# Moving loads of raw W and pieces of a mixture within the first passes of a linear-attention and expert-mixture kernel

## The chip, the cores and the metric

The kernel runs on one core of a Trainium2 chip. The metric is the device time of one execution in microseconds; the time before is the median of three runs. The profiles show one execution each. Engine names are those of the profile: PE (TensorE matmuls), PEld (its weight loads), DVE (VectorE), ACT (ScalarE), POOL (GpSimd), SP (the engine that issues most DMAs; "SPq" rows are these issues).

## The reference

There are two stages. The first is a linear-attention recurrence over 768 tokens, for 4 batches and 8 heads of width 40. The second is a mixture of 4 experts, applied to each of the 3072 rows of 320 that the first stage gives.

```python
# r, k, v, w, a, b: [4, 8, 768, 40] float32; state: [4, 8, 40, 40]
for t in range(S):
    y[:, :, t] = einsum('bhd,bhde->bhe', r_t, state)
    Sa = einsum('bhde,bhe->bhd', state, a_t)
    state = state * w_t[:, :, None, :] - einsum('bhd,bhe->bhde', Sa, b_t) \
            + einsum('bhd,bhe->bhde', v_t, k_t)
x = y.transpose(0, 2, 1, 3).reshape(3072, 320)
p = probs / (probs.sum(-1, keepdims=True) + 1e-9)          # [3072, 4]
for e in range(4):
    h = maximum(x @ w1[e], 0)                              # w1[e]: 320 x 1024
    out += p[:, e:e+1] * (h @ w2[e])                       # w2[e]: 1024 x 320
```

## The kernel before, in words

**Units and passes.** Time is cut into 12 chunks of 64 tokens. A unit is one chunk of two batches (8 heads each), so there are 24 units, u = 0 to 23. After a prologue, a loop runs passes u = 1 to 23. In the words of the change a pass is counted from one: its "fifth pass" is u = 4, "pass 6" is u = 5, and "passes 6 to 8" are u = 5, 6, 7. This text says u throughout.

**What is made of a unit.** Three generators hold its work, and a pass advances several units at once:
- `within(unit)` has all that needs no state. Raw W is turned into `G` by two DVE transposes (`turn_raw`, L241), and a scan (L419) makes running products of it. These four short DVE instructions and their scan are called the G group here. Then `pg` on PE, `gp` and its reciprocal on DVE, `n_tok`, `k_tok`, `AT` (turned from raw A), `VT` and `RT` (from raw V and raw R), and on PE `pNT`, `pKT`, `pc`, `pfe`, `pe`; DVE masks the results into `VC` and `ET`, ACT copies `F`. Its last part is `E V`, the PE group `pev`, which reads `ET`.
- `substitute` inverts triangular blocks. ACT and DVE copy `blocks` from `F`, DVE turns them into `M` (L547, 2 us), and for units from 2 on POOL runs the substitution on `Z` (L572, L585). `merge` then turns `Z` into `Qc` and `QTc` on DVE (L596, L598) and finishes the inverse with `pY` and `pQ` on PE; the last of this is what the change calls the inverse product.
- `step(unit)` is the part with the state: `prn`, then `psat`, `pxr` and `pdy` on PE, the state's update on DVE, and at the end the rows x of the mixture, transposed, as `xT`. From chunk 2 on xT is placed by twelve SBUF-to-SBUF DMAs (L736) that SP issues.

**The mixture.** Chunk 0 is done unit by unit (`mixture_of_unit`), later chunks by two units at a time (`mixture_of_chunk`, 256 rows). Each is a list of entries in `todo`: `ups` computes h = relu(x w1) of one half of an expert, `down` or `down_1` and `down_2` multiply by w2. `ups` works on a piece of w1, loaded by three DMAs (L300) into one of two buffers `w1p` (some into `sums`), and consists of `up_last` (the last 64 of the 320 channels: 8 small matmuls, PE tile names `ph`) and `up_main` (the other 256; also `ph`), after which ACT takes both PSUM tiles through the relu (L770). The second product uses seven half-size products instead of eight: `add_h` forms five sums of h on DVE (`a`, L880), and PE makes `p431` in `down_1`, and `p75` and `p26` in `down_2` (all "p" in the profile). DVE adds these into `osb` (L784, L786), with `gate` and `minus_gate`.

**PSUM.** All `ph`, `po` and `p` tiles have one tag, `mm`, with three buffers that go round. A `ph` pair takes two of them, `p431`, `p75` and `p26` one each, so the second `ph` tile after a `p75`, `p26` pair takes the buffer of that `p75`. The attention's tiles have another tag with five buffers.

**What sets the order.** `gap(n)` calls `mix`, which runs the next one or two entries of `todo`; with `pieces` given it runs that many. `lead()` runs the `up_last` of the next entry ahead of its time if that entry has a `lead`. After the program is written, a scheduler orders each engine's instructions by its own costs, except those kept in program order; `in_order[0]` keeps all matmuls of a pass in program order. In passes with `early` (u below EARLY = 5) the order of the parts is another than later. Each engine's queue is then fixed and runs in order, SP's with its DMA issues too.

**Raw W.** `load_raw(unit, "W")` makes four DMA issues into a single buffer for all units, `rawW`; the next unit's may start when DVE has turned the one before. In pass u it is for unit u + 3.

The lines in question, in the loop:

```python
        if u + 3 < NU:
            go(load_raw(begin(u + 3), "WA"))
            load(units[u + 3], "WBKV")
            later.extend(load_raw(units[u + 3], "VR"))
```

Of the kernel before, what the change touches and what calls it, by code (L numbers as in the profile page):

```python
# [15 lines left out]
def kernel(  # L16
# [41 lines left out]
    E, DM, F = moe_w1.shape  # L58
    P = 128
# [5 lines left out]
    NU = NC * B // 2  # L65
    DT = DM - 2 * P

    in_order = [False]
# [6 lines left out]
    def matmul(**k):  # L75
        return stated(nc.tensor.matmul(**k))  # L76
# [104 lines left out]
    EARLY = 5  # L181
# [4 lines left out]
    units = []  # L186

    def begin(u):
        q = Unit()
        q.u, q.c, q.bp = u, u // (B // 2), u % (B // 2)  # L190
        q.b = [2 * q.bp, 2 * q.bp + 1]
        q.start, q.end = q.c == 0, q.c == NC - 1
        q.apart = u >= EARLY + 2
        q.n = {}
        units.append(q)
        return q
# [9 lines left out]
    def load_raw(q, names):  # L206


        moves = []
        for x in names:  # L210
            q.n["raw" + x] = t = raw[x]()
            heads = srcs[x].rearrange("b h t e -> (b h) t e")[q.b[0] * H:(q.b[1] + 1) * H, q.c * L:(q.c + 1) * L, :]
            heads = heads.rearrange("n (x two) e -> x n (two e)", two=2)
            for r in range(2):
                if x in "RV":

                    sets = ((slice(0, 8, 2), slice(r, 16, 4)), (slice(1, 8, 2), slice(3 - r, 16, 4)))
                else:
                    sets = ((slice(0, 8), slice(r, 16, 2)),)
                for n, hs in sets:  # L220
                    for y, w_ in enumerate((D + Q, 2 * D - Q)):
                        o = slice(64 * r + Q * y, 64 * r + Q * y + Q)
                        moves.append(lambda eng, out=t[o, n, 0:w_], in_=heads[:, hs, Q * y:Q * y + w_]: eng.dma_start(out=out, in_=in_))  # L223
        return moves
# [10 lines left out]
    def go(moves, eng=None):  # L235
        for move in moves:
            move(eng or nc.sync)
# [65 lines left out]
    def used(n):  # L303

        while len(pieces) < n_pieces:
            k = len(pieces)
            if k in in_sums:
                before = k - 5 if k >= 5 else -1
            else:
                at = [x for x in range(k) if x not in in_sums]  # L310
                before = at[-2] if len(at) > 1 else -1
            if before >= n:
                break
            load_piece()

    def load_w2(e):
        tc.keep_in_program_order(nc.sync.dma_start(out=w2_sb[e][:], in_=moe_w2[e].rearrange("(f p) d -> p f d", p=P)))
# [425 lines left out]
    def up_last(k, xT, n):  # L743

        w1 = pieces[k]
        ph = [ps.tile([P, HF // 2, n], FP32, name="ph", tag="mm", bufs=3) for _ in range(2)]

        for f in range(HF // 2):
            for c in range(2):
                for i in range(2):  # L750
                    matmul(
                        out=ph[i][half(c), f, :], lhsT=w1.last[part(i), f, half(c)],
                        rhs=xT[part(i), 2, :], start=(f == 0), stop=False,
                    )
        return ph

    def up_main(k, xT, n, ph):

        w1 = pieces[k]
        h = sb.tile([P, HF, 2 * P], FP32, name="hs", tag="hs", bufs=3)  # L760
        for i in range(2):
            for f in range(HF // 2):
                for g in range(2):
                    at = i * HF // 2 + f
                    matmul(
                        out=ph[i][:, f, :], lhsT=w1.main[:, g, at * P:(at + 1) * P],
                        rhs=xT[:, g, :], start=False, stop=(g == 1 and f == HF // 2 - 1),
                    )
        for i in range(2):
            nc.scalar.activation(  # L770
                out=h[:, i * HF // 2:(i + 1) * HF // 2, 0:n], in_=ph[i][:], func=ACTF.Relu,
            )
        return h

    def up(k, xT, n):
        return up_main(k, xT, n, up_last(k, xT, n))

    def scale(q, e, minus=False):
        return (minus_gate if minus else gate)[:, q.c, q.bp, e:e + 1]

# [15 lines left out]
    def mixture_of_unit(q):  # L796

        hs, at = {}, 2 * E * q.u

        def ups(e):  # L800
            hs[e] = [up(at + 2 * e + x, q.xT, P) for x in range(2)]
            used(at + 2 * e + 2)
            if q.u == 0 and e + 2 < E:
                load_w2(e + 2)

        def down(e):
            po = ps.tile([P, DM], FP32, name="po", tag="mm", bufs=3)
            for f in range(NF):
                matmul(
                    out=po[:], lhsT=hs[e][f // HF][:, f % HF, 0:P], rhs=w2_sb[e][:, f, :],  # L810
                    start=(f == 0), stop=(f == NF - 1),
                )
            if e == 0:
                q.osb = outputs()
            add(q.osb[:], po[:], scale(q, e), e == 0)
            if e == E - 1:
                stores.append(lambda: store(q, q.osb))

        todo.append(lambda: ups(0))
        for e in range(E):  # L820
            todo.append(lambda e=e: down(e))
            if e + 1 < E:
                todo.append(lambda e=e: ups(e + 1))

# [119 lines left out]
    todo, last, later, stores = [], [], [], []  # L946

    def begin_later(n):
        for move in later[:n]:
            tc.keep_in_program_order(move(nc.sync))  # L950
        del later[:n]

    def mix(n):

        for piece in todo[:n]:
            ready = stores[:]
            del stores[:]
            piece()
            for begin_store in ready:
                begin_store()  # L960
            begin_later(3 if n > 1 else 6)
        del todo[:n]

    def lead():
        if todo and hasattr(todo[0], "lead"):
            todo[0].lead()

    def run(gen, n=99):
        if gen is None:
            return  # L970
        for _ in range(n):
            if next(gen, gen) is gen:
                break
# [95 lines left out]
    sparse = range(4 * 1, 4 * 4 + 2)  # L1069
# [2 lines left out]
    sums_at.update({4 * 4 + 3: 2, 4 * 5 + 0: 3, 4 * 5 + 1: 2, 4 * 5 + 2: 3})  # L1072
    sum_ops = (None for e in range(E) for _ in add_weights(e))
    for u in range(1, NU):
        in_order[0] = u < EARLY
        q = units[u]
        m = s_next = w = w_next = iter(())
        if u + 1 < NU:
            m, s_next = merge(units[u + 1]), begin_step(u + 1)
            w_next = ws[u + 1]  # L1080
        if u + 2 < NU:
            w = ws[u + 2]

        def gap(n, pieces=None):
            at = 4 * u + n
            run(sum_ops, sums_at.get(at, 0))
            mix((1 if at in sparse else 2) if pieces is None else pieces)

        early = u < EARLY
        if early:  # L1090
            begin_later(len(later))
        run(w_next, 99 if early else 1)
        run(s, 1)
        gap(0)


        if early:
            run(s, 1)
        run(w, 1)
        if not early:  # L1100
            run(w_next)
            run(s)

        if early:
            run(w, 1)
            gap(1)
            run(s)
        if u == 1:
            mixture_of_unit(q)
        elif q.bp:  # L1110
            mixture_of_chunk(units[u - 1:u + 1], chunks_x[q.c])
        if not early:
            begin_later(len(later))
            run(w, 1)
            run(m, 1)
            gap(1)

        if u + 3 < NU:
            go(load_raw(begin(u + 3), "WA"))
            load(units[u + 3], "WBKV")  # L1120
            later.extend(load_raw(units[u + 3], "VR"))
        run(w, 2)

        soon = u in (2, 3, 4)
        if soon:
            run(w, 1)
        if early:
            run(m, 1)
        else:
            run(s_next, 1)  # L1130
            run(m, 1)
        if soon:
            substitute(units[u + 2], nc.gpsimd)
        gap(2)

        if not early:
            run(m, 1)
        if not soon:
            run(w, 1)
        if not early:  # L1140
            lead()
            run(s_next, 1)
        if not soon and u + 2 < NU:
            substitute(units[u + 2], nc.gpsimd)
        if early:
            run(w, 1)
        if u + 3 < NU:
            ws.append(within(units[u + 3]))
            run(ws[u + 3], 1)
        if early:  # L1150
            run(m, 1)
            run(s_next, 1)
            run(m)
            gap(3, 1)
            run(s_next, 1)
            mix(0 if 4 * u + 3 in sparse else 1)
        else:
            gap(3)
        s = s_next
# [31 lines left out]
```

## Time and profile before

| | us |
|---|---|
| median of three runs (1123.12 to 1125.46) | 1123.36 |
| the profiled execution | 1122.36 |
| its span, first to last instruction | 1120.2 |
| PE busy | 1076.8 |
| DVE busy | 757.0 |
| POOL busy | 501.9 |
| ACT busy | 353.2 |
| mean granted PE clock | 0.986 |

The span is what the views divide; the profiled execution is 2.16 us longer than its span. Shares of busy time are averages over the whole span, and a busy PE is not PE at its peak. A row of the timeline gives start, duration, engine, line, operation, out<-in and shapes; in brackets stands the idle time of the engine just before, and what ended it. A row of the windows view gives a stretch, its length, and for each engine its busy time in it and the number of instructions, then the mean PE clock, the DMA share and GB/s. Passes begin on PE at about 95 us (u = 1), 129 (u = 2), 161 (u = 3), 191 (u = 4), 233 (u = 5), 280 (u = 6), 329 (u = 7) and 372 (u = 8); from there on a pass takes about 43 us.

### The profile page before, as it was taken

How to read it: one execution, taken by the hardware profiler on the slowest of the kernel's cores; microseconds unless marked ns; L12 is line 12 of the kernel's file. 1: busy time of each engine (PE TensorE's matmuls, PEld its weight loads, DVE VectorE, ACT ScalarE, POOL GpSimd, SP SyncE). 2: the span in 40 equal slices, each digit the busy share in tenths (PEclk: the TensorE clock that was granted, in tenths of full speed). 3: DMA queues.
4: the chain of work that ended last, by engine and by line, in shares of the span. 5: the costliest groups of instructions: out<-in, count | busy, mean ns of one | idle time of the engine just before them, and what ended most of it. 6: DMA issues, size and time to landing. Idle time of an engine off the chain costs nothing.

```text
span 1120.2 us, 38531 instructions
## 1 busy us (share of the span) xinstructions
PE 1076.8 (96%) x16100; PEld 961.0 (86%) x16100; DVE 757.0 (68%) x1553; ACT 353.2 (32%) x956; POOL 501.9 (45%) x1272
## 2 busy tenths in 40 slices
PE   6888899898989999999999999999999999999998
PEld 5777777787978989989999998989989899988887
DVE  8665588886657767767767677677677686543343
ACT  2322444233332332333332432342332333321110
POOL 5004676761625635636536437437346346340000
PEclk8899999999999999999999999999999999999999
DMA  7785536335353454553544543543543542231330
GB/s 116 203 250 139 124 68 152 80 95 121 81 110 93 122 126 97 130 123 82 128 99 101 129 107 86 143 100 88 143 106 87 129 103 64 77 90 60 107 90 12
DMA packets 268869, 122.18 MB, mean 109 GB/s; under 512 B 213737, under 2 KB 242073, under 8 KB 268697
## 3 DMA queue, kind: packets, MB, share of 16 engines
q1 hardware_dynamic: 265416, 119.12, 44.0%
q8 instruction: 127, 2.08, 0.8%
q10 hardware_dynamic: 3280, 0.61, 0.3%
q14 instruction: 46, 0.37, 0.1%
HBM read 111.79 MB, written 3.93 MB: 103 GB/s over the span
## 4 chain that ended last, share of the span: by engine, by line
PE 59%; POOL 12%; DVE 9%; issue 5%; ACT 4%; SPq 2%; DMA 2%; DVEq 0%; POOLq 0%
PE ph L76 26%; PE p L76 20%; POOL Z L585 8%; POOL Z L572 4%; PE psat L76 2%; PE pdy L76 2%; DVE M L547 1%; SPq L223 1%; PE pxr L76 1%; PE po L76 1%; PE pfe L76 1%; PE pQ L76 1%; DVE G L419 1%; ACT Yq L619 1%; PE prn L76 1%
## 5 line engine op out<-in xcount | busy, mean ns | idle before, releaser
L76 PE MATMUL ph<-xT,w1p 128*128 128x256 f32 (+3 forms) x3040 | 446.0, 378 | 7.8 <-issue 7.8
L76 PEld LDWEIGHTS ph<-xT,w1p 64*64 64x64 f32 (+1 forms) x3040 | 338.3, 162 | 76.6 <-issue 33.8
L585 POOL TENSOR_TENSOR Z<-Z 128x31 f32<-128x31 f32 (+7 forms) x704 | 259.1, 368 | 55.2
L880 DVE TENSOR_TENSOR a<-hs 128x512 f32<-128x512 f32 x220 | 152.3, 710 | 105.9 <-ACT hs L770 105.9
L572 POOL TENSOR_TENSOR Z<-M,Z 128x62 f32<-128x62 f32 (+7 forms) x352 | 145.8, 414 | 139.0 <-DVE M L563 113.2
L770 ACT ACTIVATE hs<-ph 128x512 f32<-128x512 f32 (+1 forms) x208 | 115.0, 564 | 214.5 <-PE ph L76 213.4
L76 PE MATMUL p<-sums,a 128*128 128x160 f32 x1056 | 164.8, 299 | 0.0
L76 PEld LDWEIGHTS p<-sums,a 128*128 128x128 f32 x1056 | 152.9, 190 | 2.2
L786 DVE SCALAR_TENSOR_TENSOR osb<-p,gate,osb 128x320 f32<-128x320 f32 (+1 forms) x243 | 108.1, 482 | 60.3 <-PE p L76 56.9
L544 POOL COPY below<-F 32x256 f32<-32x256 f32 x48 | 24.0, 501 | 221.0 <-ACT F L502 219.5
L76 PE MATMUL p<-w,a 128*128 128x160 f32 x704 | 106.2, 301 | 1.3 <-ACT hs L770 0.8
L76 PE MATMUL p<-w,hs 128*128 128x160 f32 x704 | 102.9, 299 | 0.0
L76 PEld LDWEIGHTS p<-w,a 128*128 128x128 f32 x704 | 98.3, 190 | 4.4 <-ACT hs L770 4.4
L76 PEld LDWEIGHTS p<-w,hs 128*128 128x128 f32 x704 | 100.2, 190 | 2.2
L604 POOL COPY QT<-QTc 32x256 f32<-32x256 f32 x96 | 50.3, 524 | 75.2 <-DVE QTc L598 35.1
L547 DVE STREAM_TRANSPOSE M<-blocks 128x1024 f32<-128x1024 f32 x24 | 47.3, 1971 | 39.5 <-ACT blocks L541 39.4
L692 ACT COPY RS<-pxr 64x256 f32<-64x256 f32 x88 | 32.4, 368 | 108.5 <-DVE SX L400 43.3
L529 ACT COPY EV<-pev 64x160 f32<-64x160 f32 x96 | 23.5, 287 | 93.4 <-PE pev L76 93.0
L432 DVE RECIPROCAL gp<-gp 128x320 f32<-128x320 f32 x24 | 51.6, 2151 | 0.7
L596 DVE STREAM_TRANSPOSE Qc<-Z 128x256 f32<-128x256 f32 x24 | 15.0, 627 | 46.4 <-POOL Z L585 46.3
L619 ACT COPY QT<-pQ 32x128 f32<-32x128 f32 x96 | 24.7, 257 | 58.9 <-PE pQ L76 57.2
L651 ACT COPY SN<-prn 128x256 f32<-128x256 f32 x44 | 15.0, 371 | 80.4 <-DVE RH L646 77.6
(147 smaller groups left out, 1371.0 us busy)
## 6 DMA issues: line engine op xcount, KB each, us to landing
w1p<-in_moe_w_dram SPq DMA_DIRECT2D x95, 512.0 KB
w1p<-in_moe_w_dram SPq DMA_DIRECT2D x190, 64.0 KB
w<-in_moe_w_dram SPq DMA_DIRECT2D x4, 1280.0 KB
sums<-in_moe_w_dram SPq DMA_DIRECT2D x9, 512.0 KB
natW<-in_w_dram SPq DMA_DIRECT2D x48, 80.0 KB
natB<-in_b_dram SPq DMA_DIRECT2D x48, 80.0 KB
natK<-in_k_dram SPq DMA_DIRECT2D x48, 80.0 KB
out_dram<-osb SPq DMA_DIRECT2D x46, 80.0 KB
```

Of the source, the lines that this page charges most:

```text
L76: return stated(nc.tensor.matmul(**k))
L432: pin(nc.vector.reciprocal(out=gp[:], in_=gp[:]))
L544: tc.keep_in_program_order(nc.gpsimd.tensor_copy(out=q.below[quarter(i)], in_=q.F[quarter(i), :, 0:Q]))
L547: ins = nc.vector.transpose(out=M[:], in_=cols)
L572: ins = eng.tensor_tensor(out=Z[:, 1:3, 0:n, j + 1:Q], in0=M[:, j:j + 2, None, j + 1:Q].to_broadcast([P, 2, n, m]), in1=Z[:, here, 0:n, j: ...
L585: eng.tensor_tensor(out=z[:, 0], in0=z[:, 0], in1=z[:, x], op=ALU.add)
L604: ins = nc.gpsimd.tensor_copy(out=q.QT[quarter(i), :, quarter(i % 2)], in_=QTc[quarter(i)])
L619: nc.scalar.copy(out=of_slot(to[quarter(2 * r)], y), in_=src)
L692: nc.scalar.copy(out=RS[half(s), x ^ s::2], in_=prs[x][half(s)].rearrange("p (j i) t -> p j i t", i=2),)
L770: nc.scalar.activation(out=h[:, i * HF // 2:(i + 1) * HF // 2, 0:n], in_=ph[i][:], func=ACTF.Relu,)
L786: nc.vector.scalar_tensor_tensor(out=to, in0=p, scalar=sc, in1=to, op0=ALU.mult, op1=ALU.add)
L880: nc.vector.tensor_tensor(out=t[:], in0=x, in1=y, op=op)
```

## The change

- For u = 5, 6, 7 raw W of unit u + 3 is begun at the head of the pass; raw A keeps its place.
- In the unit-wise mixture `ups` becomes an entry with a `lead`, and for u = 1 to 4 `lead()` is called at the head of the pass. This puts the next piece's `up_last` ahead of `pev`.
- In u = 4 `gap(1)` runs two entries instead of one, and the one entry at the end of that pass is dropped.
- `in_order` holds for u = 5 too.

```diff
-    def up(k, xT, n):
-        return up_main(k, xT, n, up_last(k, xT, n))
-
...
         def ups(e):
-            hs[e] = [up(at + 2 * e + x, q.xT, P) for x in range(2)]
-            used(at + 2 * e + 2)
-            if q.u == 0 and e + 2 < E:
-                load_w2(e + 2)
+            ph = []
+
+            def lead():
+                if not ph:
+                    ph.append(up_last(at + 2 * e, q.xT, P))
+
+            def piece():
+                lead()
+                hs[e] = [up_main(at + 2 * e, q.xT, P, ph[0])]
+                hs[e].append(up_main(at + 2 * e + 1, q.xT, P, up_last(at + 2 * e + 1, q.xT, P)))
+                used(at + 2 * e + 2)
+                if q.u == 0 and e + 2 < E:
+                    load_w2(e + 2)
+
+            piece.lead = lead
+            return piece
...
-        todo.append(lambda: ups(0))
+        todo.append(ups(0))
         for e in range(E):
             todo.append(lambda e=e: down(e))
             if e + 1 < E:
-                todo.append(lambda e=e: ups(e + 1))
+                todo.append(ups(e + 1))
...
-        in_order[0] = u < EARLY
+        in_order[0] = u <= EARLY
...
         if early:
             begin_later(len(later))
+        ahead = u + 3 < NU and u in range(EARLY, EARLY + 3)
+        if ahead:
+            go(load_raw(begin(u + 3), "W"))
+        if early:
+            lead()
         run(w_next, 99 if early else 1)
         run(s, 1)
         gap(0)
...
         if early:
             run(w, 1)
-            gap(1)
+            gap(1, 2 if u + 1 == EARLY else None)
             run(s)
...
         if u + 3 < NU:
-            go(load_raw(begin(u + 3), "WA"))
+            go(load_raw(units[u + 3] if ahead else begin(u + 3), "A" if ahead else "WA"))
             load(units[u + 3], "WBKV")
             later.extend(load_raw(units[u + 3], "VR"))
...
             gap(3, 1)
             run(s_next, 1)
-            mix(0 if 4 * u + 3 in sparse else 1)
         else:
             gap(3)
```

In the order as built, these moves show:
- On PE, from u = 1 to u = 4, eight `ph` matmuls stand before `pev` instead of after `pxr`. In u = 4 a whole `ph` piece stands before `pNT` instead of after `pfe`, the next one before `pY` instead of before `psat`, and `p431` before `psat` instead of after it. From the `ph` in u = 5 on PE's order is the same.
- On DVE, in u = 5, 6, 7, the G group stands right after `k_tok`, ahead of `RT` and `Qc`, instead of after the additions to `w` and `sums` (u = 5), after `RH` (u = 6) and around `QTc` (u = 7).
- On SP, the four issues of raw W stand before the weight piece that precedes the second half of raw R. In u = 4 the three issues of one weight piece stand in front of the last three of the twelve xT issues.
- POOL's order is the same.

## Prediction

> **What bounds the kernel now.** I read the page first: engine totals, clock row, and the chain that ended last.
>
> ```profile
> PE 1076.8 (96%) x16100; PEld 961.0 (86%) x16100; DVE 757.0 (68%) x1553; ACT 353.2 (32%) x956; POOL 501.9 (45%) x1272
> ...
> PE 59%; POOL 12%; DVE 9%; issue 5%; ACT 4%; SPq 2%; DMA 2%; DVEq 0%; POOLq 0%
> ```
>
> PE is busy 96% of the span, so this kernel gets shorter only where PE stands still or runs at half clock. I therefore listed PE's idle stretches in the timeline. Between 90 us and the end, those of over 0.4 us, but for one of 0.44 at 489, all lie before 364 us, in u = 1 to 7, the passes that the change touches. Then I asked for the busy time of each engine in the stretches with a gap, and in one like the late ones without a gap (406.27 to 415.18, u = 8):
>
> ```profile
> core 0: us, PE busy (x) PEld busy (x) DVE busy (x) ACT busy (x) POOL busy (x), PEclk, DMA share, GB/s
> 94.00:98.80 4.80, 2.14 (x69) 1.49 (x70) 4.55 (x10) 0.24 (x2) 1.31 (x5) 1.00 0.60 160
> ...
> 160.64:163.94 3.30, 2.87 (x161) 2.63 (x164) 0.55 (x1) 2.05 (x8) 2.67 (x9) 1.00 0.05 11
> ...
> 201.30:221.27 19.97, 16.80 (x198) 15.14 (x196) 19.17 (x36) 4.19 (x9) 13.62 (x35) 0.91 0.37 81
> 265.88:279.90 14.02, 11.01 (x130) 9.55 (x122) 10.75 (x19) 5.11 (x15) 2.85 (x7) 0.88 0.66 150
> 313.51:328.58 15.07, 11.02 (x131) 9.52 (x123) 10.98 (x19) 5.11 (x16) 2.06 (x5) 0.89 0.52 125
> 362.19:372.40 10.21, 9.43 (x131) 8.23 (x123) 7.24 (x13) 5.11 (x15) 2.38 (x5) 1.00 0.65 157
> 406.27:415.18 8.91, 8.91 (x134) 8.10 (x127) 5.80 (x10) 5.16 (x16) 1.83 (x5) 1.00 0.60 134
> ```
>
> The rows from 265.88, 313.51 and 362.19 hold the instructions of the last row (`ph`, `psat`, `ph`, `p`) in u = 5, 6, 7: 14.02, 15.07 and 10.21 us instead of 8.91. The excess is 5.1, 6.15 and 1.3 us, part PE standing still, part PEclk below 1. The page calls the releaser "issue", so I followed the first in the timeline:
>
> ```profile
> 249.18 9.80 SPq L736 DMA_DIRECT2D xT<-Y  x12
> ...
> 259.08 1.65 SPq L300 DMA_DIRECT2D w1p<-in_moe_w_dram  x3
> 260.77 1.56 SPq L223 DMA_DIRECT2D rawW<-in_w_dram  x3
> 264.11 0.93 DVE L241 STREAM_TRANSPOSE G<-rawW 128x256 f32<-128x256 f32 x2 [5.37 <-DMA rawW<-in_w_dram]
> ...
> 266.57 1.26 DVE L880 TENSOR_TENSOR a<-hs 128x512 f32<-128x512 f32 x2
> 269.01 0.37 DVE L786 SCALAR_TENSOR_TENSOR osb<-p,minus_gate,osb 128x160 f32<-128x160 f32 x1
> 269.49 0.87 PE L76 MATMUL ph<-xT,w1p 64*64 64x256 f32 x11 [3.01 <-issue]
> ```
>
> Raw W's last three moves stand on SP behind twelve `xT` moves and a weight piece. DVE waits 5.37 us for them at `G`, and behind `G` wait the `a` sums and the `osb` additions that read `p75` out of PSUM. The tag `mm` has three buffers, so the second `ph` tile takes p75's: the `minus_gate` addition ends at 269.38, PE goes on at 269.49. In u = 6 it is the same link (DVE idle 7.98 before `G`, PE 4.05). In u = 7 DVE waits 3.64 for raw A, PE 0.78.
>
> **What the Trainium skill says.** "PSUM — Partial Sum Buffer", section Engine vs sequencer instructions: the Vector queue is strict FIFO. The trace agrees; the additions' `p75` was complete 5 us before they ran. "TensorE: Matmul & The Clock Gate", Part 1: after an idle window of about 3.4 us PE's clock is halved until a busy one. The trace's clock record has three drops to 0.5 between 90 us and the end, each 3.41 us long, from 209.07, 270.51 and 318.30, each after 3 us or more of gap; the 2.61 us gap at 94.9 brought none. "Perfetto Trace Analysis", Optimization Strategy: recurring bubbles can mean too few buffers; the three waits for p75 fit.
>
> **The change part by part.** No operation is added or removed on PE, DVE or POOL; all is order. Steps are in PE time of before.
>
> *Leads, u = 1 to 4.* `up_last` (8 matmuls) of the next piece moves ahead of `pev`. In u = 2, 3, 4 PE idles 0.43 us before `pxr` for ACT's SX copies (row 160.64: 3.30 minus 2.87); the lead takes about 0.6 us at 128 columns (a piece is 2.6, of which two ACT evictions 0.89 apart give 1.8 to `up_main`), 0.9 at 256, and covers it: 3 x 0.43. In u = 1 PE waits 2.61 for ET; ET doesn't move, so 0.6 of PE work slides into the gap (bounds 0.4 to 1.1). Their pieces were issued over 7 us earlier. **Sum 1.9.**
>
> *Fifth pass's piece, u = 4.* Row 201.30 holds two gaps, 2.26 (`pNT` for n_tok) and 0.91 (`pc` for RT); the half clock costs 1.15 on `pc`, `pfe`, `pe` (2.59 instead of 1.44) and 0.13 on `ph`. Removed: 4.45. Now a `ph` piece of 4.6 stands before `pNT`, from 205.2 to 209.8; n_tok is ready at 207.3, RT by 209. But every later piece moves up: PE reaches the next `ph` at 205.2 + 4.6 + 0.9 + 0.5 + 0.95 + 4.35 = 216.5, and its second tile needs p75's. The DVE order there is `M` (unmoved, 214.45 to 216.5), `osb`, memset, `a`, `Z`, `minus_gate`: 216.5 + 0.46 + 0.1 + 0.6 + 0.73 + 0.37 = 218.75. **A new wait of 2.2 us**; no raw W is behind it. Bounds: 0 if DVE comes to p75 before M, 3.9 if the clock drops for it (half of 3.41). I take 2.2, since 2.61 brought no drop. The `p` group that stood between `psat` and `pev` has moved up too, so 0.43 for SX appears at the head of u = 5. Net 4.45 - 2.2 - 0.43 = **1.8**. On SP the next piece's three issues (1.65) go in front of the last three `xT` issues; PE has freed its buffer at 209.8 and SP is there at 203.0 + 9 x 0.8 = 210.2, so SP doesn't stand. What is behind, these xT and raw W of unit 7, slips by 1.65: raw W, issued at 212.5 before, was turned at 223.4, so it has some 6 us.
>
> *Raw W early, u = 5 to 7.* Four `rawW` issues (2.6 us of SP) now come before a weight piece and the second half of rawR. Buffer: unit 7's raw W is turned at 223.4, SP gets there at 235.5. rawR slips from 238 to 243, RT needs it at 254; the piece waits for PE until 238.8 anyway. Data is in SBUF by 245, and DVE has the whole `G` group (0.93 + 0.17 + 0.07 + 1.22 + 0.3, with gaps 2.6) right after `k_tok`. Price of that place in u = 5: G to 253.2, two `osb` for p431 (done 253.06) to 254.1, RT to 254.8, while `pc` was due at 254.02: **0.8 lost** (0 to 1.0). In u = 6 RT is done at 301.1, `pc` due 301.66; in u = 7 RT 349.9, due 350.33; QTc at 302.1 and 350.95, `pY` due 303.1 and 351.8: nothing lost, by margins of 0.4 to 1.0. Then p75's last read: a sums wait for hs (262.0), 264.8 against PE's 266.7 in u = 5; 311.75 against 313.5 in u = 6; 361.9 against 362.2 in u = 7, where raw A still comes at 359.4 but two `a` sums now run ahead of it. So those waits end with their half clock: 5.1 - 0.8 = **4.3**, **6.15**, **1.3**. They cover each other: if raw W is on time, what is late next is hs on ACT, then raw A.
>
> *Order kept in u = 5.* PE's order from the `ph` at 234.23 on is that of before: 0, as the instructions match; without it the scheduler might have moved more (unknown, left out).
>
> **Sum:** 1.9 + 1.8 + 4.3 + 6.15 + 1.3 = 15.45. The profiled execution took 1122.36 (span 1120.2 and 2.16 around it), the median of the runs is 1123.36, 1.0 above. 1123.36 - 15.45 = **1107.9**.
>
> **Rivals.** *The POOL chain takes over.* POOL's inverse (21.7 us from `M`) ends just before `Qc`; before, QTc had 1.7 us to spare in u = 6 and 0.85 in u = 7. If `G` ahead of Qc delays it by its full 2.6 in all three passes, 7.8 comes back: 1115.7. For: POOL's 12% of the chain. Against: k_tok is early enough by the sums above. *Raw A replaces raw W.* Its issue stays behind xT and a piece (262.4), and AT stands in the same DVE queue; if p75 waits on it, u = 7 keeps its 1.3 and the other two about 2 each: 1113. Against: in u = 5 and 6 AT now stands behind the p75 reads. *Slower.* Raw W has one buffer, so its issue waits on SP for DVE's last turning, with weight pieces, rawR and xT queued behind. If the turning of before (223.4) came after SP's arrival (235.5), 12 us later than seen, every further us would stand in front of the pieces; from 5 us more in each of the three passes the 15 us are used up: at 7 more, 1123.4 + 21 - 15.5 = 1129. Against: the margin. *No effect:* the `a` sums, not raw W, hold p75; then 1.9 + 1.8 - 2.4 for three `G` delays, 1122.
>
> **How the numbers follow.** Forecast 0.80, POOL chain 0.08, raw A 0.08, slower 0.03, no effect 0.01. A measurement of this kernel can tell about 0.2%, 2.2 us, from no change. Faster 0.95, same 0.02, slower 0.03. The range: without the 2.2 and the 0.8 it is 1104.9, with a clock drop, the raw A wait in u = 7 and no gain from u = 1 it is 1111.5; I reach to 1113 for the raw A case and to 1104.5 below.
>
> **What would show it.** Right: windows of 8.9 us for the `ph`-to-`pe` stretch in u = 5, 6, 7; no clock drop near 270 and 318; no DVE wait on rawW there; a PE gap of about 2 before a `ph` in u = 4 ended by `minus_gate`; 0.8 before `pc` in u = 5. Wrong: "issue" gaps of 3 us left before `ph`, DVE waiting on rawA in front of `osb`, or PE waiting at `pY` for QTc.

## The result, and the profile after

The changed kernel took 1114.06 us in the median of seven executions (1109.2 to 1116.56), beside 1123.12 for the kernel before in the same session; the ratio is 0.9918, 95% interval 0.9893 to 0.9942. So it is faster by 9.1 us. The forecast was 15.45 us and 1107.9, with a range that ended at 1113.0: right in direction, 6 us too much. The profiled execution took 1112.43 us, its span is 1110.2, 10.0 shorter than before.

The page of the changed kernel, engine totals and chain that ended last:

```profile
PE 1075.2 (97%) x16100; PEld 959.7 (86%) x16100; DVE 758.1 (68%) x1553; ACT 352.9 (32%) x956; POOL 501.5 (45%) x1272
...
PE 77%; DVE 4%; POOL 3%; ACT 2%; issue 2%; SPq 2%; DMA 1%; DVEq 0%; POOLq 0%
```

PE's share of the chain rose from 59 to 77%, POOL's fell from 12 to 3, DVE's from 9 to 4. Busy PE time hardly moved (1.6 us): what went was waiting. The windows view of the changed kernel shows the stretches shown of before, and above them four of u = 1 that matter now:

```profile
core 0: us, PE busy (x) PEld busy (x) DVE busy (x) ACT busy (x) POOL busy (x), PEclk, DMA share, GB/s
94.71:98.12 3.41, 1.66 (x66) 1.54 (x67) 3.23 (x10) 0.68 (x4) 1.67 (x6) 1.00 0.72 194
98.12:101.54 3.42, 3.42 (x20) 3.20 (x22) 1.75 (x4) 0.81 (x4) 2.87 (x8) 0.50 0.58 201
111.78:115.19 3.41, 1.49 (x34) 1.25 (x37) 2.96 (x5) 1.51 (x3) 2.78 (x9) 1.00 0.36 69
115.19:118.60 3.41, 3.41 (x47) 3.08 (x39) 1.84 (x4) 0.07 (x1) 1.70 (x8) 0.50 0.66 104
202.87:222.84 19.97, 18.67 (x221) 16.07 (x220) 19.29 (x38) 4.07 (x9) 13.24 (x35) 1.00 0.42 108
267.33:276.39 9.06, 9.06 (x130) 8.28 (x120) 6.11 (x10) 5.09 (x15) 1.80 (x5) 1.00 0.60 134
310.20:319.45 9.25, 9.25 (x130) 8.23 (x123) 6.89 (x13) 5.11 (x16) 2.02 (x5) 1.00 0.64 141
353.06:362.93 9.87, 9.44 (x131) 8.24 (x123) 6.90 (x13) 5.10 (x16) 2.05 (x5) 1.00 0.64 157
```

The last three rows are the ph-to-pe stretch of u = 5, 6, 7: 9.06, 9.25 and 9.87 us instead of 14.02, 15.07 and 10.21, with a full clock. The first four rows were not foreseen: two windows at half clock in u = 1, at 98.12 and 115.19, where the profile of before has none. Each follows a window in which PE was busy for only 1.66 and 1.49 us of 3.41.

From the timeline of the changed kernel, PE's waits that are left and that the forecast spoke of:

```profile
96.40 0.94 PE L76 MATMUL pev<-VC,ET 64*64 64x40 f32 x29 [2.00 <-DVE ET L400]
...
114.79 0.84 PE L76 MATMUL pc<-RT,VT 40*64 40x64 f32 x32 [1.92 <-DVE RT L241]
...
133.36 0.69 PE L76 MATMUL pxr<-RT,SaT 64*64 64x64 f32 x30 [0.19 <-ACT SX L672]
...
220.31 4.74 PE L76 MATMUL ph<-xT,w1p 64*64 64x256 f32 x30 [1.30 <-issue]
...
255.44 0.69 PE L76 MATMUL pc<-RT,VT 40*64 40x64 f32 x32 [0.94 <-DVE RT L241]
...
354.09 0.87 PE L76 MATMUL ph<-xT,w1p 64*64 64x256 f32 x11 [0.43 <-issue]
```

The next table shows where the difference of the profiles arises (us, after minus before). A pass is counted here from its `pg` on PE to the `pg` of the next pass:

| stretch | forecast | changed kernel | raw W alone (first experiment) |
|---|---|---|---|
| up to the head of u = 1 | 0 | -1.1 | -1.1 |
| head of u = 1, to its `pg` | -0.6 | +1.1 | +1.6 |
| u = 1, 2, 3 | -1.3 | +1.6 | -0.4 |
| u = 4 | -1.8 | -1.2 | +0.7 |
| u = 5 | -4.3 | -3.9 | -5.0 |
| u = 6 | -6.15 | -5.6 | -5.8 |
| u = 7 | -1.3 | -0.3 | -0.1 |
| u = 8 to 11 | 0 | -0.4 | -0.6 |

A half-clock window more or less moves a row by about 1.5 us (worked out below), so the experiments were read by stretch and by clock, not by the median alone.

### The profile page after: what moved, and what is told of

It reads as the page before. It is cut to its first block, busy times and chain, and to the rows that moved or that the text cites. A ratio compares the mean times of both kernels' runs of the same rounds, so it can differ in the third digit from the quotient of the medians.

```text
span 1110.2 us, 38530 instructions
## 1 busy us (share of the span) xinstructions
PE 1075.2 (97%) x16100; PEld 959.7 (86%) x16100; DVE 758.1 (68%) x1553; ACT 352.9 (32%) x956; POOL 501.5 (45%) x1272
## 4 chain that ended last, share of the span: by engine, by line
PE 77%; DVE 4%; POOL 3%; ACT 2%; issue 2%; SPq 2%; DMA 1%; DVEq 0%; POOLq 0%
PE ph L76 34%; PE p L76 27%; PE pdy L76 2%; POOL Z L585 2%; PE psat L76 2%; PE pxr L76 2%; PE prn L76 1%; PE po L76 1%; PE pfe L76 1%; POOL Z L572 1%; PE pQ L76 1%; PE pc L76 1%; PE pev L76 1%; PE pe L76 1%; PE pY L76 1%
## 5 line engine op out<-in xcount | busy, mean ns | idle before, releaser
L572 POOL TENSOR_TENSOR Z<-M,Z 128x62 f32<-128x62 f32 (+7 forms) x352 | 148.5, 422 | 130.1 <-DVE M L563 104.2
```

What stands on the lines that cost most here:

```text
L572: ins = eng.tensor_tensor(out=Z[:, 1:3, 0:n, j + 1:Q], in0=M[:, j:j + 2, None, j + 1:Q].to_broadcast([P, 2, n, m]), in1=Z[:, here, 0:n, j: ...
```

## The experiments

Two theories stood at the start. **Theory:** raw W is nearly the whole gain; the leads and the moved piece bring 1 to 2 us; half-clock windows in u = 1 took some 3 us. **Rivals:** A, the order kept in u = 5 carries the gain; B, leads and moved piece cost more than they bring.

**Raw W alone.** The kernel before with this:

```diff
+        ahead = u + 3 < NU and u in range(EARLY, EARLY + 3)
+        if ahead:
+            go(load_raw(begin(u + 3), "W"))
...
-            go(load_raw(begin(u + 3), "WA"))
+            go(load_raw(units[u + 3] if ahead else begin(u + 3), "A" if ahead else "WA"))
```

> The kernel before with one part of the change alone: raw W of unit u + 3 begun at the head of u = 5, 6, 7. Theory (raw W is nearly the whole gain; leads and fifth pass's piece bring 1 to 2 us between them, and 3 us of the shortfall are half-clock windows in u = 1 and 2 that have nothing to do with raw W): 9.5 us faster than before (3.9 + 5.6 + 0.4 less some 0.4 for a scheduler that is free in u = 5), about 1113.5; windows of 9 us for the ph-to-pe stretch in u = 5, 6, DVE still waiting for raw A in u = 7. Rival A (the order kept in u = 5, not raw W, carries it): under 6 us faster. Rival B (leads and the moved piece cost more than they bring): 10.5 us faster or more, ahead of the changed kernel.

Measured: 1112.77 us (six executions), ratio 0.9920 [0.9890, 0.9951]: as much as the whole change brings. PE's waits of this kernel between 85 and 600 us (total, times, longest):

```profile
PE pev L76 <- DVE ET L400: 2.6, 1, 2.6
PE pNT L79 <- DVE n_tok L468: 2.2, 1, 2.2
PE pc L76 <- DVE RT L241: 1.7, 2, 1.2
PE pQ L76 <- ACT Yq L619: 1.3, 1, 1.3
PE pxr L76 <- ACT SX L672: 1.3, 3, 0.4
PE ph L76 <- issue: 0.7, 1, 0.7
```

The 7.8 us of `ph` on "issue" are down to 0.7, that of u = 7. And there is no wait before `pc` in u = 5: DVE turns RT there at 251.43 and begins `G` only at 254.68. The 0.8 us that the forecast charged to raw W belong to another part of the change.

**Without raw W.** The changed kernel with those lines put back.

> The changed kernel with raw W put back to its old place. Theory: the 9 to 10 us are gone again, so 0 to 2.5 us faster than before (1.3 for the leads, 1.2 for the fifth pass's piece, less what half-clock windows in u = 1, 2 take), with PE standing 3 to 4 us before a ph in u = 5 and u = 6 and a half-clock window after each. Rival A (the order kept in u = 5 carries the gain of u = 5): the gap of u = 5 is gone here too, so 4 us faster than before or more. Rival B (leads and the moved piece cost): slower than before by 0.5 us or more.

Measured: 1121.05 us (22 executions), ratio 0.9988 [0.9972, 1.0003]. The other parts together make no difference that shows. The old waits are back, with the order of u = 5 kept. Timeline of PE:

```profile
269.92 0.87 PE L76 MATMUL ph<-xT,w1p 64*64 64x256 f32 x11 [1.84 <-issue]
316.17 0.89 PE L76 MATMUL ph<-xT,w1p 64*64 64x256 f32 x11 [3.21 <-issue]
361.93 0.87 PE L76 MATMUL ph<-xT,w1p 64*64 64x256 f32 x11 [1.15 <-issue]
```

Rival A's 4 us did not come, so the order kept in u = 5 does not carry the gain. But u = 5 takes 44.41 us here, 47.16 before and 43.27 in the changed kernel: 2.75 us of the gain of u = 5 come without raw W. The wait is 1.84 us instead of 3.01, and no half-clock window follows it, as the border of two windows at 269.1 cut it in two. In u = 6 most of the gain is raw W's (47.82 us here, 48.68 before, 43.04 in the changed kernel).

**Without leads.** The changed kernel without the call of `lead()` at the heads of u = 1 to 4.

> The changed kernel without the leads at the heads of u = 1 to 4. Theory: 0.6 us more in u = 1 and 0.24 in each of u = 2, 3, 4 where SX stands open again, so 1.3 us slower than the changed kernel (about 1115.3), whatever the half-clock windows do, which come and go from one execution to the next. Rival B (the leads brought the half-clock windows of u = 1 and 2, by splitting PE's idle time otherwise): 2 us faster than the changed kernel (about 1112), no half-clock window between 90 and 130 us, and shares of clock above those of the changed kernel by 0.002 in all executions.

Measured: 1115.11 us (12 executions), ratio 0.9939 [0.9921, 0.9957]: the median that the theory named, but not its reason. From `pg` of u = 1 to `pg` of u = 2 it took 33.4 us instead of 35.6, with no half-clock window at 115, as rival B said; but one at 98.67 is there, and the mean clock of all executions is only 0.0007 higher, not 0.002. The time is lost later, in u = 6 and 7, where `ph` waits 1.60 and 1.37. DVE of this kernel in u = 6:

```profile
308.85 0.71 DVE L241 STREAM_TRANSPOSE AT<-rawA 128x512 f32<-128x512 f32 x1 [6.25 <-DMA rawA<-in_a_dram]
```

The scheduler has put `AT` ahead of the `a` sums, so that DVE waits for raw A there. This is the rival "raw A replaces raw W" of the prediction; the changed kernel escapes it in u = 6 by an order that nothing in the code asks for.

**Without the moved piece.** The changed kernel with the piece of u = 4 back at the end of the pass.

> The changed kernel with the piece of u = 4 put back to the end of the pass. Theory: the 2.26 and 0.91 us before pNT and pc come back with the half-clock window (1.2 to 1.3) near 208, less the 1.30 before ph and 0.42 before pxr, so 1.5 us slower than the changed kernel with the window and about 0.8 without it (1115). Rival (the second ph's wait for p75 in u = 4 eats the gain whole): no difference, within 0.3 us in the pg-to-pg time of u = 4 and 5.

Measured: 1113.14 us (seven executions), ratio 0.9922 [0.9894, 0.9950]: no slower than with it. u = 4 took 41.3 us (with a half-clock window at 210) instead of 40.6, u = 5 took 42.2 instead of 43.3: what the piece wins in u = 4 it gives back in u = 5. The wait of 0.94 before `pc` in u = 5 isn't there without it.

**VT first.** What remained was why u = 1 took 2 us longer with leads. Before, DVE turned VT ahead of `n_tok` there:

```profile
110.19 0.65 DVE L241 STREAM_TRANSPOSE VT<-rawV 128x512 f32<-128x512 f32 x1
110.77 0.70 DVE L468 SCALAR_TENSOR_TENSOR n_tok<-natB,gp 128x320 f32<-128x320 f32 x1
...
114.34 0.69 PE L76 MATMUL pc<-RT,VT 40*64 40x64 f32 x32 [1.48 <-DVE RT L241]
```

DVE of the changed kernel there, and then of a kernel in which VT of unit 3 is turned ahead of `n_tok` in the program and pinned to that place:

```profile
108.35 2.15 DVE L432 RECIPROCAL gp<-gp 128x320 f32<-128x320 f32 x1
110.54 0.60 DVE L468 SCALAR_TENSOR_TENSOR n_tok<-natB,gp 128x320 f32<-128x320 f32 x1
...
112.28 0.67 DVE L241 STREAM_TRANSPOSE VT<-rawV 128x512 f32<-128x512 f32 x1
...
114.04 0.70 DVE L241 STREAM_TRANSPOSE RT<-rawR 128x512 f32<-128x512 f32 x1
```

```profile
107.28 2.15 DVE L432 RECIPROCAL gp<-gp 128x320 f32<-128x320 f32 x1
109.35 0.66 DVE L241 STREAM_TRANSPOSE VT<-rawV 128x512 f32<-128x512 f32 x1
109.93 0.60 DVE L473 SCALAR_TENSOR_TENSOR n_tok<-natB,gp 128x320 f32<-128x320 f32 x1
...
112.74 0.70 DVE L241 STREAM_TRANSPOSE RT<-rawR 128x512 f32<-128x512 f32 x1
```

```diff
+        if q.u == PADDED:
+            VT = sb.tile([P, 2 * NJ, L], FP32, name="VT", tag="turned", bufs=3)
+            pin(turn_raw(VT[:], n["rawV"][:]))
         q.K, q.N = k_tok(), n_tok()
```

> The changed kernel with DVE's order in u = 1 put back by hand: VT turned between the reciprocal and n_tok instead of behind AT; PE's, SP's, ACT's and POOL's orders untouched. Theory (the leads shifted the scheduler's order on DVE, that made RT later, and the longer wait of PE tips the window over): the wait before pc falls from 1.92 to about 1.25 us, the half-clock window at 115 goes, the pass u = 1 is 33.5 instead of 35.6 us, 2 us faster than the changed kernel (1112). Rival (the lead itself, whose 8 matmuls move PE's idle time, brings the window): wait 1.25, but the window stays, 0.6 us faster.

Measured: 1110.79 us (six executions), ratio 0.9892 [0.9862, 0.9923]. RT starts 5.46 us after the reciprocal's start instead of 5.69, and the reciprocal 2.42 after `pg` instead of 2.65, so the wait before `pc` is 1.46 instead of 1.92 (1.25 expected). There is no half-clock window at 115, and u = 1 takes 33.55 us instead of 35.6. The median is 3.3 us below that of the changed kernel, though the two intervals overlap.

That one profile does not show alone that VT is the reason. The clock goes by windows of 3.41 us on a fixed grid (last section), and here a border of two windows lies at 113.14: it would have cut a wait of 1.92 us too, into 1.1 and 0.8. What holds wherever the border lies is the size. With 1.46 us no window can hold more idle time than that around `pc`, and between 85 and 400 us no full-clock window with less than 1.51 was followed by half clock. With 1.92 us, by an estimate from the trace of the changed kernel, about half of the places of the border leave 1.75 us or more in one window, and all 16 such windows were followed by half clock. All three profiles with leads, VT behind AT and nothing filled have the window at 115 (the changed kernel, without raw W, without the moved piece), with 1.84 to 1.92 us of idle time ahead of it; none of the profiles of other kernels has it.

**Filled.** To price the windows alone, PE multiplies the identity by itself where it stands idle: in the changed kernel 5 times ahead of `pev` and 7 times ahead of `pc` in u = 1, and with raw W alone 11 times ahead of `pev` in u = 1 (shown here) and 14 times ahead of `pNT` in u = 4.

```diff
+        p = banks("pev")
+        if q.u == 2:
+            fill(p[0][:, 0:P], 11)
```

> The changed kernel with 5 idle-time matmuls (identity by identity, into the bank that the next group overwrites) ahead of pev and 7 ahead of pc in u = 1. They use time in which PE stands anyway, so the stalls stay and only PE's idle share falls. Theory (of the missing gain some 3 us are half-clock windows of 3.41 us in u = 1, which follow any window in which PE idled over about 1.6 us): idle falls to about 1.2 and 1.0 us in the two windows, no half-clock window between 90 and 130 us, 2.5 to 3 us faster than the changed kernel, about 1111, mean clock up by 0.003. Rival (the half clock is a side show that costs PE little, since PE waits for DVE in these passes anyway): within 0.7 us of the changed kernel.

> Raw W alone, with 11 idle-time matmuls ahead of pev in u = 1 and 14 ahead of pNT in u = 4; all other engines' orders as with raw W alone. Theory: the half-clock windows at 98 and at 207 to 214 go, the stalls stay; 1.4 us for the first, 1.4 to 2.8 for the one or two behind pNT: about 1109.5, 3.3 us faster than raw W alone and 4.5 faster than the changed kernel, with a mean clock of 0.990 or more. Rival (windows cost little): 1112.5 to 1113, as raw W alone.

Measured: the changed kernel filled 1110.37 us (six executions; ratio 0.9888 [0.9860, 0.9915]), raw W alone filled 1108.38 (six; 0.9872 [0.9843, 0.9901]), with no half-clock window between 90 us and the end but one in the last microseconds. They are 3.7 and 4.4 us below their unfilled kernels, where the theory had 2.5 to 3 and 3.3; the intervals of each pair overlap. The clock explains a part: over all executions it is higher by 0.0009 and 0.0032 (the theory had 0.003 for the first), which is 0.9 and 3.0 us at the price worked out below. Where the rest of the first difference comes from is not shown. The multiplications cost more than I had counted: one is two matmuls in the trace and takes 0.22 us, so that 14 of them take 3.1 us ahead of `pNT`, which comes 0.7 later than with raw W alone. Raw W alone, filled, has the lowest median of all kernels here, with instructions that compute nothing; its interval overlaps those of the other filled kernels and of VT first.

**Raw A.** Two tries to take PE's last wait in u = 7, on top of raw W alone: raw A of unit 9 at the head of u = 6, then that of unit 10 at the head of u = 7.

> Raw W alone, and in u = 6 raw A of unit 9 too is issued at the head of the pass, behind raw W, so that it no longer stands behind xT in SP's queue. Theory (in u = 7 raw A, through AT ahead of the a sums and p75's additions in DVE's queue, holds the second ph tile): DVE's wait for raw A and PE's 0.67 us before ph in u = 7 go, about 0.7 us faster than raw W alone, 1112. Rival (raw A has one buffer, so the early issue waits on SP for DVE's turning of unit 8, and weight pieces and xT behind it come late): PE waits over 1 us in u = 6 or 7, 1 us slower or more.

> Raw W alone, and in u = 7 raw A of unit 10 too at the head of the pass, behind raw W (the run before moved that of u = 6, which is not the one that AT waits for in u = 7). Theory (raw A behind xT in SP's queue holds AT, and with it the a sums and p75's additions): DVE's wait for raw A in u = 7 (3.55 us) goes, PE's 0.67 before ph too; u = 7 in 43.0 us instead of 43.7; about 0.7 faster than raw W alone, 1112. Rival (AT takes another place on DVE, ahead of RT, Qc and QTc, and holds those): a wait of 0.5 us or more before pc or pY in u = 7, nothing won.

Measured: 1112.27 us (six; 0.9899 [0.9871, 0.9928]) and 1113.64 (nine; 0.9915 [0.9887, 0.9942]). The first took neither wait of u = 7 away: DVE's for raw A is 3.95 us (3.55 with raw W alone), PE's before `ph` 1.07 (0.67). I had moved the wrong unit's raw A. In the second, DVE's wait for raw A and PE's before `ph` are gone, but DVE has `AT` and `G` ahead of `RT`, which ends at 345.03, and PE waits for it:

```profile
344.32 0.71 DVE L241 STREAM_TRANSPOSE RT<-rawR 128x512 f32<-128x512 f32 x1
```

```profile
345.18 0.69 PE L76 MATMUL pc<-RT,VT 40*64 40x64 f32 x32 [0.71 <-ACT KT L454]
```

(The profile names KT; RT ended 0.15 us before PE went on.) u = 7 took 43.54 us instead of 43.71: one wait in the place of another, as the rival said.

**Two combinations.** The changed kernel without the moved piece, VT first, filled ahead of `pev` and `pNT`; and the changed kernel with VT first, filled ahead of `pev`.

> The changed kernel without its second part in u = 4 (the piece goes back to the end of the pass), with VT first on DVE in u = 1, and with 8 idle-time matmuls ahead of pev in u = 1 and 14 ahead of pNT in u = 4. Theory (what the moved piece of u = 4 wins is the time it fills, and it pays for it with the waits before ph and pxr in u = 4 and before pc in u = 5, so that 14 matmuls without use do as well as the piece): u = 4 and 5 take 82.7 us together, as with raw W alone and filled, against 83.7 with the piece; 1107 to 1108.5 in all. Rival (the moved piece is worth its 1.8 us): 84 us or more for the two passes, 1110.

> The changed kernel with VT first on DVE in u = 1 and 8 idle-time matmuls ahead of pev in u = 1; no other order moves. Theory: the half-clock window at 98, which comes with that wait in about half of the executions, is gone in all of them; 1109 to 1110 with a narrower spread, 4 to 5 us faster than the changed kernel, which leaves u = 1 to 4 about 0.7 us faster than raw W alone and filled, and u = 5 about 1 us slower. Rival (the spread has another source): as with VT first alone, 1110.8, from 1108 to 1113.

Measured: 1110.64 us (six; 0.9878 [0.9848, 0.9909]) and 1111.61 (six; 0.9886 [0.9857, 0.9915]). Both missed their numbers. In the first, u = 4 and 5 took 83.56 us, between the two expectations: some 0.9 was lost in u = 4 around `psat`, which waited for QT, and the orders of DVE and ACT had moved again, so it doesn't tell the two apart. The second was no faster than VT first without filling; its profile has no half-clock window between 90 us and 1110, but two at 42 and 70 us, in the prologue. The spread is not from u = 1 alone, as the rival said.

**The clock over all executions.** Each execution has a mean clock beside its time. Over the 158 executions of the 13 kernels that have a clock on record (59 of them before), with one constant for each kernel, a regression gives 0.86 us of time (standard error 0.045) for each us of clock lost, that is of 1115 us times (1 - clock). A half-clock window loses 1.7 us of clock, so it costs 1.5 us. At equal clock, against before, with 95% intervals: without raw W -0.3 (+-0.7), without leads -3.3 (+-0.9), changed kernel -6.0 (+-1.1), raw W alone -6.6 (+-1.2), VT first -7.3 (+-1.3). So leads and moved piece together bring nothing over raw W alone that shows. That the kernel without leads is slower at equal clock fits the waits of 1.60 and 1.37 us that AT's place brought there. The changed kernel's mean clock is 0.9876, that of before 0.9840; 0.0036 x 1115 x 0.86 = 3.5 us. So of the gain some 6 us are stalls and 3.5 are clock.

## Why the prediction was right or wrong

**Right: the bound, the link and its size.** Raw W's late issue held p75's buffer through DVE's queue. The prediction gave 5.1, 6.15 and 1.3 us of excess in the three passes; raw W alone brings 5.0 and 5.8 in u = 5 and 6, and without it the waits are back, though the one of u = 5 is shorter. The "Trainium skill", page "PSUM — Partial Sum Buffer", section Engine vs sequencer instructions, has the strict order of the Vector queue that this rests on; the waits of 1.84 and 3.21 us that come back without raw W agree.

**Wrong, the step that counted most: the leads, 1.9 us of gain.** By the stretches above, the head of u = 1 and u = 1 to 3 took 2.7 us more than before instead of 1.9 less, a miss of 4.6 that is most of the error. It has three parts.
- *The half clock.* The prediction took "the 2.61 us gap at 94.9 brought none" for a property of the gap. It was luck. The windows stand on a grid of 3.41 us; in the profile of before a border at 96.43 cut that gap into 1.5 and 1.1 us. With raw W alone the gap is as long, but the borders lay at 94.74 and 98.15, and the window between them had 1.77 us of idle time; in the changed kernel, where the lead has shortened the gap to 2.0, it had 1.75. Both were followed by half clock. That half-clock window, worth about 1.5 us, is not due to the change. The three drops of before were misread too: the one at 209.07 did not follow "3 us or more of gap", but a wait of 2.26 us and a window with 2.29 us of idle time.
- *DVE's order in u = 1.* The prediction held it for unmoved. The scheduler put VT behind AT, so RT came later, and the wait before `pc` grew from 1.48 to 1.92. The longer wait, and in this profile the half-clock window at 115 with it, made u = 1 2 us longer. The wait is due to the change, since putting VT back shortens it to 1.46; the window takes a border of the grid in the wrong place besides.
- *SX.* Of 0.43 us in u = 2 and 3 there is 0.19 left: PE goes on 2.35 us after psat's start in both kernels, when ACT is done, and the lead at 128 columns takes only 0.47 us. In u = 4 there is 0.55. Without a window the leads are worth 0.44 at the head of u = 1 (15.27 us with VT first from the second half of `pc` to `pg`, against 15.70 before), and about 0.1 at each of the three heads that follow: from `psat` to `pg` it takes 10.29, 10.29 and 9.60 us with VT first, and 10.38, 10.38 and 9.72 without leads.

**Wrong in its place: the moved piece of u = 4, net 1.8.** The gaps of 2.26 and 0.91 and the half clock went as worked out; the wait for p75 came, 1.30 instead of 2.2 (DVE's chain behind `M` took 1.95 instead of 2.3, and PE came later); the 0.42 before `pxr` came. In u = 4 that left 1.2. But the 0.8 before `pc` in u = 5 (0.94 measured), which the prediction charged to raw W's `G`, comes with this piece: it isn't there with raw W alone or without the piece. Without leads but with the piece it is there again, at 1.60. Over u = 4 and 5 the piece nets nothing: 83.68 us with it (VT first), 83.56 without it though that one carries a half-clock window.

**Wrong in size: u = 7, 1.3 us.** It brought 0.1 to 0.4. "Two `a` sums now run ahead" of AT was misread: that order is that of u = 6. In u = 7 AT stands ahead of the sums and of p75's last read, and raw A still comes at 350:

```profile
349.99 0.71 DVE L241 STREAM_TRANSPOSE AT<-rawA 128x512 f32<-128x512 f32 x1 [3.27 <-DMA rawA<-in_a_dram]
...
353.61 0.38 DVE L783 SCALAR_TENSOR_TENSOR osb<-p,minus_gate,osb 128x160 f32<-128x160 f32 x1
```

PE goes on at 354.09, 0.1 us behind that read. The rival "raw A replaces raw W" had named this for u = 7; I gave it 0.08. That AT stands behind the reads of p75 in u = 6 was misread as well: it stands ahead of the last of them (at 308.47, after 1.57 us of waiting for raw A; the read ends at 310.51), but PE did not come to wait for it.

**Not needed.** The POOL chain did not take over: no wait for QTc before `pY` appears. Rival A fell as well. What the order kept in u = 5 does by itself was not tried.

**What stays open.** Why some windows in the prologue, between 16 and 74 us, are at half clock in one execution and not in the next; what the moved piece would be worth in an order of DVE without `G` ahead of RT in u = 5, which was not tried; and which of the other parts brings the 2.75 us of u = 5 that come without raw W.

## What to carry to other kernels

When a change moves instructions that a scheduler places, compare the order of every engine, and in every pass: here two waits that took back part of the gain, before `pc` in u = 1 and in u = 5, came from DVE orders that no line of the change mentions. Do not infer from one profile that a stall of some length leaves the clock alone; take the clock and the time of all executions, and compare kernels at equal clock. Where PE has to stand, shortening or splitting a stall can be worth more than the time it saves, since the next window's clock hangs on the idle time in this one.

## What the runs showed of the hardware

- Half-clock windows stand on a grid of 3.41 us: the drops of before at 209.07, 270.51 and 318.30 are 18 and 14 times 3.413 us apart. The phase of the grid differs from one profile to the next. The "Trainium skill", page "TensorE: Matmul & The Clock Gate", Part 1, speaks of an idle window; here a window needs only about half of it idle. In the ten profiles whose grid a drop after 50 us fixes, from 85 to 400 us, all 16 full-clock windows in which PE idled 1.75 us or more were followed by a half-clock one, 2 of the 7 with 1.50 to 1.69 us, and none with less.
- That count is not the whole rule. In the prologue a window with only 1.00 us of idle time was followed by a half-clock one, at 42.83 us (VT first, filled).
- A window already at half clock can be followed by a second one with less idle time still: after 0.31, 0.82 and 0.79 us behind `pNT` in u = 4 (raw W alone, and the two with raw A), and in the prologue after none at all (from 57.71 us without leads, 59.25 with raw W filled, 58.71 with raw A of u = 7). But after 0.44 us, at 209.07 before, the clock came back. What decides between them is not shown.
- Executions of one kernel differ with the clock: the 59 of before go from 1118.3 to 1130.1 us, at mean clocks from 0.979 to 0.988, and 0.009 x 1115 x 0.86 is 8.6 of these 11.8 us. That the place of the grid sets the clock of an execution fits the profiles, but is not shown: there is one trace of each kernel.
